# A quarter of a Q projection moved into seven-product runs, with the helper sums spread out to make room

## The chip, the cores and the metric

One core of one Trainium2 chip. The metric is the device time of one execution in microseconds (us). Each trace is of one execution. Engines: PE is TensorE (PEld its weight loads), DVE is VectorE, ACT is ScalarE, POOL is GpSimd, SP issues most transfers.

## The reference, cut to what matters

```python
def _A_ref(x, wqkv, wo):                       # x: 2048 tokens x 1024
    q, k, v = split(x @ wqkv)                  # 32 heads of 32
    phi = lambda t: jnp.where(t > 0, t + 1, jnp.exp(t)) + 1e-6
    pq, pk = phi(q), phi(k)
    kv = einsum("bhsd,bhse->bhde", pk, v)      # linear attention
    o = einsum(pq, kv) / (einsum(pq, pk.sum(s)) + 1e-6)
    return o @ wo
h = x + _A_ref(_layernorm(x), wqkv, wo)
h2 = h + mlp_over_tokens(_layernorm(h), w1, b1, w2, b2)   # 2048 -> 3584 -> 2048, gelu
```

The change lies in `x @ wqkv` and what surrounds it. The MLP, which takes more than half of the time, it leaves alone except in the last microseconds. Its two matrix products are called Mixer 1 (with w1) and Mixer 2 (with w2, also "the second MLP" below); psI are the accumulators of their inner products, hst the statistics of a block of h, and tp a transposed block.

## The kernel before: the parts that the change touches

A block product of 2x2 blocks normally takes 8 products. The kernel computes most of K and V in "runs" of 7 products (p1 to p7), at the price of sums of blocks: four of the weights (`w_sums`, T1 to T4, made once) and four of the tokens (`x_sums`, made for each pair of token blocks). All of these sums are VectorE's. TensorE accumulates into four buffers (psA, psB, psC, psE); results of different products are added on VectorE. The Q projection is plain: 32 "units" of 8 matmuls of 512 columns, some used as filler in the first run and the rest in a stage behind the K and V runs.

```python
def x_sums(q):                                    # 4 additions of 128x512 on VectorE
    a11, a12, a21, a22 = x_blocks(q)
    sm = spool.tile([P, 4, hk2, P], FP16, tag="xs", name="xs")
    pin(nc.vector.tensor_tensor(sm[:, 0], a21, a22, ALU.add))
    pin(nc.vector.tensor_tensor(sm[:, 1], sm[:, 0], a11, ALU.subtract))
    ...                                           # cut: sm[:, 2], sm[:, 3]
def p6(self): self.mm(self.B, self.s2, self.t2, False)   # needs sm[:, 1] and T2

def run_step(n, prev, after6=None, after5=None, after7=None, fill=None):
    n.p1()                                        # n: this run, prev: the run before
    prev.late22(); prev.p3(); prev.dve22(); prev.p4()
    n.p6()
    prev.dve21()
    if after6 is not None: after6()               # norm statistics of a later token block
    n.p2(); n.p5()
    prev.late12()                                 # Exp and Relu on ScalarE
    n.dve11()
    prev.dve12()                                  # last phi of the run before, on VectorE
    if after5 is not None: after5()
    n.p7()                                        # includes an addition on VectorE
    if after7 is not None: after7()               # x_sums of the next pair, after V runs
```

`pin` keeps an instruction in the order in which it is written. What is not pinned, such as the plain Q units in the first run, the builder may move. Accumulators outside the runs come from a ring of five buffers, handed out in turn, one for each call of `acc_tile`.

## Time and profile before

| | before |
|---|---|
| time, median of 3 | 560.86 us (560.84 to 561.08) |
| span of the profiled execution | 559.3 us |
| a K+V pair of runs | 13.03 us |
| first K run's first product starts at | 41.23 us |
| first Mixer 1 product (after the output projection) starts at | 234.10 us |
| last w2 load of the second MLP, issue to landing | 503.17 to 510.9, 7.8 us |
| start of the last group of psC matmuls to the end of the span | 7.70 us |

TensorE is the bound; the prediction below shows the lines for that. The short list of all that TensorE waited for (us in total, times, longest):

```profile
PE acc_t L98 <- DVE warm L88: 1.2, 1, 1.2
PE psB L945 <- DVE xs L931: 0.3, 1, 0.3
PE tp L1112 <- DVE xn L848: 0.2, 1, 0.2
```

The first is the program's start. There is one short wait on a token sum (at 34.31 us), one on a normalised block, and nothing else in 559 us.

### The profile page before, as it was taken

To read this page: it belongs to the slowest core of one execution; us is meant where nothing else is said; L and a number is where in the kernel's file an instruction comes from. 1 tells how busy PE (TensorE), PEld (TensorE's weight loads), DVE (VectorE), ACT (ScalarE), POOL (GpSimd) and SP (SyncE) were. 2 spreads that over 40 slices of the span, in tenths; PEclk is the share of its full clock that TensorE was granted. 3 is DMA by queue.
4 is the path that set the end of the run, shared out by engine and by line. 5 is a ranking of instruction groups with operands and counts; after the bars stand their busy time and mean duration, and the time that the engine had idled before them with its cause. 6 is when DMAs were issued, how large, how long until landed. Compare 5 with 4: busy or idle time off the path is not lost.

```text
span 559.3 us, 8827 instructions
## 1 busy us (share of the span) xinstructions
PE 553.0 (99%) x3339; PEld 316.2 (57%) x3339; DVE 435.3 (78%) x848; ACT 291.1 (52%) x617; POOL 28.0 (5%) x38
## 2 busy tenths in 40 slices
PE   8999999999999999999999999999999999999996
PEld 3444444454444444456766766666444667667664
DVE  6898888544777688889989789887997879749745
ACT  5747677766767877646456465464210413413222
POOL 1000000000000000000000000000002103103112
PEclk9999999999999999999999999999999999999999
DMA  9933342115774762102240440413869649849334
GB/s 306 297 76 76 80 90 39 19 36 203 223 203 136 241 202 76 75 1 85 69 150 5 147 134 18 151 46 88 206 203 237 197 137 245 206 131 229 86 95 66
DMA packets 83627, 74.25 MB, mean 133 GB/s; under 512 B 15602, under 2 KB 76032, under 8 KB 83584
## 3 DMA queue, kind: packets, MB, share of 16 engines
q1 hardware_dynamic: 78528, 69.09, 41.1%
q0 software_dynamic: 4384, 3.95, 5.3%
q10 hardware_dynamic: 672, 0.66, 0.3%
q8 instruction: 26, 0.43, 0.3%
q14 instruction: 17, 0.14, 0.1%
HBM read 58.86 MB, written 11.67 MB: 126 GB/s over the span
## 4 chain that ended last, share of the span: by engine, by line
PE 97%; DVE 2%; ACT 1%; issue 0%; DVEq 0%
PE psI L230 25%; PE acc_t L230 18%; PE psC L230 16%; PE psB L230 8%; PE psB L945 4%; PE psC L945 4%; PE psA L945 4%; PE acc_t L869 2%; PE acc_t L1231 2%; PE psB L342 2%; PE psA L342 2%; PE psE L945 2%; PE psC L342 2%; PE psA L230 1%; PE kvps L898 1%; PE psE L342 1%
## 5 line engine op out<-in xcount | busy, mean ns | idle before, releaser
L230 PEld LDWEIGHTS <-is 128*128 128x128 f16 x736 | 71.8, 98 | 31.2 <-DVE hi L230 0.4
L230 PEld LDWEIGHTS <-sa 128*128 128x128 f16 x606 | 59.2, 98 | 27.1
L230 PEld LDWEIGHTS <-wq 128*128 128x128 bf16 (+1 forms) x496 | 48.5, 98 | 28.1 <-issue 1.0
L230 PE MATMUL acc_t<-wo_sb,pqT 128*128 128x512 f16 x256 | 55.6, 379 | 0.0
L488 POOL DMA_DIRECT2D out_dram<-wq x30 | 26.1, 927 | 525.4 <-ACT wq L491 495.0
L230 PE MATMUL acc_t<-xnT,wq_sb 128*128 128x512 bf16 x192 | 43.4, 379 | 0.0
L230 PEld LDWEIGHTS <-pqT 128*128 128x128 bf16 x256 | 25.0, 98 | 30.5 <-issue 0.6
L193 DVE TENSOR_SCALAR e_sb<-e_sb 128x512 bf16<-128x512 bf16 x64 | 18.6, 290 | 28.7 <-ACT e_sb L189 28.1
L230 DVE TENSOR_TENSOR t<-psI,t 128x256 f32<-128x256 f32 (+1 forms) x45 | 20.8, 475 | 22.2 <-PE psI L230 20.9
L189 ACT ACTIVATE e_sb<-acc_t 128x512 bf16<-128x512 f32 x40 | 23.9, 597 | 24.5 <-PE acc_t L230 12.0
L230 PE MATMUL psC<-gs,wq 128*128 128x512 f16 x140 | 34.1, 379 | 0.0
L945 PEld LDWEIGHTS <-xs 128*128 128x128 f16 x208 | 20.0, 98 | 23.4 <-DVE xs L931 1.3
L230 PEld LDWEIGHTS <-wq_sb 128*128 128x128 bf16 x192 | 18.5, 98 | 23.0 <-issue 1.3
L230 PE MATMUL psC<-hT,sa 128*128 128x512 f16 x112 | 31.2, 379 | 0.0
L230 PE MATMUL psI<-hi,is 128*128 128x256 f16 x200 | 30.0, 273 | 0.0
L230 PE MATMUL psB<-hT,sa 128*128 128x512 f16 x112 | 29.7, 379 | 0.0
L230 DVE BATCH_NORM_STATS2 hst<-acc_t 128x6 f32<-128x512 f32 x32 | 21.4, 692 | 9.0 <-ACT h_bf L230 8.9
L945 PE MATMUL psA<-wkv,xnT 128*128 128x512 bf16 x104 | 26.7, 379 | 0.0
L945 PEld LDWEIGHTS <-xnT 128*128 128x128 bf16 x156 | 15.2, 98 | 18.5 <-issue 0.2
L230 PE MATMUL psC<-hT,wq 128*128 128x512 f16 x96 | 24.6, 379 | 0.0
L230 ACT CAST h_bf<-acc_t 128x512 bf16<-128x512 f32 x32 | 18.4, 582 | 11.9 <-PE acc_t L230 11.5
L230 ACT COPY psI<-psI 128x256 f32<-128x256 f32 x50 | 18.0, 360 | 11.6 <-PE psI L230 9.7
(229 smaller groups left out, 1090.2 us busy)
## 6 DMA issues: line engine op xcount, KB each, us to landing
wq<-in_B_w_dram SPq DMA_DIRECT2D x14, 1024.0 KB, 8.0
wq<-in_B_w_dram SPq DMA_DIRECT2D x12, 896.0 KB, 7.1
gs<-parked SPq DMA_DIRECT2D x9, 896.0 KB, 4.6
xr<-in_A_x_dram SPq DMA_DIRECT2D x16, 256.0 KB, 5.9
rdb<-rd_dram SPq DMA_DIRECT2D x32, 128.0 KB, 3.8
out_dram<-h_bf SPq DMA_DIRECT2D x16, 256.0 KB, 2.0
x_sb<-in_A_x_dram SPq DMA_DIRECT2D x15, 256.0 KB, 3.0
out_dram<-wq POOLq DMA_DIRECT2D x30, 128.0 KB, 4.7
```

The costliest lines, as they stand in the source:

```text
L189: pin(nc.scalar.activation(e_sb[:], src, ACT.Exp))
L193: pin(nc.vector.tensor_scalar(e_sb[:], e_sb[:], 1.0, PHI_EPS, ALU.min, ALU.add))
L230: return (lambda *a, **kw: pin(op(*a, **kw))) if self.always or getattr(Held, self.key) else op
L342: pe.matmul(ps[:, cols], lhsT=lhs[:, k, :], rhs=mv(k)[:, cols], start=(start and k == 0), stop=(k == self.nk - 1), skip_group_check=True,)
L488: nc.gpsimd.dma_start(to, ot[:, a:b], accum_op=ALU.add)
L869: mm = nc.tensor.matmul(pp[:, 0:CW], lhsT=xnT[:, kt, i * P:(i + 1) * P], rhs=wkv[:, kt, c * CW:(c + 1) * CW], start=(kt == 0), stop=(kt == ...
L898: pin(nc.tensor.matmul(kv_ps[b][:, sl, :], lhsT=pks[i % NPK][:, j * P:(j + 1) * P], rhs=vaugs[i % NVA][:, j, :], start=False, stop=(i == N ...
L945: pin(nc.tensor.matmul(ps[:], lhsT=lhs[:, k, :], rhs=rhs[:, k, :], start=(start and k == 0), stop=(k == hk2 - 1), skip_group_check=True,))
L1231: nc.tensor.matmul(qp[:, 0:SW], lhsT=wq_sb[:, kt, j * P:(j + 1) * P], rhs=xnT[:, kt, u * SW:(u + 1) * SW], start=(kt == 0), stop=(kt == ND ...
```

## The change

The intent: make tokens 1024 to 1535 of Q with seven products too, as two Q runs beside the K and V runs of q = 5 in the code, with Q's weight sums made one at a time, behind p7's addition in the K runs of four pairs. For buffer room T1 is written over the weight block that it is made from, and later buffers share memory. To save ScalarE work, a Q run's second phi takes its Relu inside a VectorE operation ("lean"). The last two stores by accumulating DMA become a fetch, an addition and a plain store.

```diff
-    for out, a, b in ((t1, b12, b11), (t2, b22, t1), (t3, b22, b12), (t4, b21, t2))[part]:
+    for out, a, b in ((t3, b22, b12), (t1, b12, b11), (t2, b22, t1), (t4, b21, t2))[part]:
     # cut: t1 is now a view of b12 itself; shared_sb holds sums, later rd, rdb and xr
+class QRun(KRun):                  # cut: 2 x (7 x 4 x 2) matmuls of 256 columns
+    lean = True
 def run_step(...):
     ...
     prev.late12()
     n.dve11()
-    prev.dve12()
     after5()
     n.p7()
+    prev.dve12()
     after7()
-q_units = [(u, j) for u in range(NSC) for j in range(ND)]
+q_units = [(u, j) for u in (0, 1, NSC - 1) for j in range(ND)]
+q_sums = {2: slice(0, 1), 3: slice(1, 2), 4: slice(2, 3), 5: slice(3, 4)}
-    for R in (KRun, VRun):
+    runs = [KRun(q), VRun(q)]
+    if q == 5:
+        runs = [runs[0], QRun(q // 2, 0), runs[1], QRun(q // 2, 1)]
+    # after7 of K runs: w_sums(qmov, q_sums[q]); of the second Q run: x_sums(q + 1, ...)
+if q == 6: ...                     # reload of the half of wq that was overwritten
-sums_at, ahead = (11, 13, 17, 19, 21), first_sums()
-scale_at = {7: (0, 0), 8: (0, 1), 15: (1, 0), 16: (1, 1), 23: (2, 0)}
+sums_at, ahead = (9, 11, 12, 13, 15), first_sums()
+scale_at = {7: (0, 0), 8: (0, 1), 14: (1, 0)}
     # cut: order of the denominators and scalings in the output stage; the tail
```

## The prediction

> **What bounds the kernel now.** I read the engine totals first, then the 40 slices, then who waited for TensorE, then the order of time in the two places where TensorE was not full.
>
> ```profile
> span 559.3 us, 8827 instructions
> ...
> PE 553.0 (99%) x3339; PEld 316.2 (57%) x3339; DVE 435.3 (78%) x848; ACT 291.1 (52%) x617; POOL 28.0 (5%) x38
> ...
> PE   8999999999999999999999999999999999999996
> ...
> PE 97%; DVE 2%; ACT 1%; issue 0%; DVEq 0%
> ```
>
> TensorE is busy 99% of the span and 97% of the chain that ended last. A busy TensorE need not be at its peak, so I checked spacing in the chain in order of time: 16 matmuls of 128x512 take 3.45 us (216 ns each), 8 of 128x256 take 0.87 us (109 ns each). Those are even spacings with no holes, and the granted clock is 1.00 everywhere. So time comes off only where TensorE gets fewer columns, and goes on wherever TensorE is made to wait. The second thing to know is where it waits already:
>
> ```profile
> 26.00:36.00 10.00, 9.72 (x57) 4.86 (x56) 9.39 (x16) 4.66 (x11) 0.00 (x0) 1.00 0.41 83
> 50.60:63.60 13.00, 13.00 (x73) 6.42 (x72) 10.56 (x25) 9.62 (x21) 0.00 (x0) 1.00 0.36 80
> 102.00:115.00 13.00, 13.00 (x74) 6.40 (x72) 6.77 (x17) 8.89 (x17) 0.00 (x0) 1.00 0.10 18
> 135.00:178.20 43.20, 43.20 (x217) 19.24 (x217) 30.04 (x64) 32.08 (x61) 0.00 (x0) 1.00 0.61 180
> 178.20:235.00 56.80, 56.80 (x270) 25.52 (x269) 45.59 (x93) 41.30 (x97) 0.00 (x0) 1.00 0.43 146
> ```
>
> After the window and its length the columns are PE, PEld, DVE, ACT, POOL, clock, DMA. Only the first stretch (start of the seven-product runs) has a TensorE hole, 0.28 us, and VectorE is 94% busy there. The others, a K+V pair early, a K+V pair late, the stage of plain Q units, and the output stage, have TensorE full and VectorE at 81, 52, 70 and 80%.
>
> In order of time there (start, duration, engine, source line, operation, output and inputs, shapes; in brackets the idle time before it and what ended it):
>
> ```profile
> 26.86 1.22 DVE L919 TENSOR_TENSOR wo_sb<-wkv 128x2048 f16<-128x2048 bf16 x1
> 28.11 1.23 DVE L919 TENSOR_TENSOR wo_sb<-wkv,wo_sb 128x2048 f16<-128x2048 bf16 x1
> ...
> 30.70 1.17 DVE L919 TENSOR_TENSOR wo_sb<-wkv 128x2048 f16<-128x2048 bf16 x1
> 31.79 1.22 DVE L919 TENSOR_TENSOR wo_sb<-wkv,wo_sb 128x2048 f16<-128x2048 bf16 x1
> ...
> 33.83 0.42 DVE L931 TENSOR_TENSOR xs<-xs,xnT 128x512 f16<-128x512 f16 x1
> ...
> 34.31 1.04 PE L945 MATMUL psB<-wo_sb,xs 128*128 128x512 f16 x4 [0.28 <-DVE xs L931]
> ```
>
> VectorE makes four V weight sums, then the token sums, and product 6 of the first V run starts the moment the second token sum ends. That is the spot with no slack at all.
>
> **What the Trainium skill says.** "TensorE: Matmul & The Clock Gate", Back-to-back issue gap, gives N/2.4 + 2.5 ns warm: 216 ns for 512 columns, 109 for 256. The trace agrees with both; it does not agree with the same section's 131 ns for sustained 512-column streams. Step-by-step there says matmuls stay in program order and only weight loads are pulled ahead; so a matmul that waits for VectorE holds all behind it, unless the instruction stream was ordered otherwise when it was built. "VectorE: DVE Perf Modes", Side-by-side, gives about 1224 ns for a two-tensor operation on 2048 16-bit elements; the weight sums take 1.22 to 1.23 us. "ScalarE: Activation LUTs", What ACT_TABLE_LOAD costs, gives 186 + 0.833 N ns with overlap of some 93 ns: 0.61 us each, 0.52 apart, at N = 512; here Exp takes 0.60 and follow-ons start 0.49 to 0.54 apart.
>
> **The change, part by part.**
> 1. Products. A quarter of Q is 8 units of 8 matmuls of 512 columns: 64 x 216 = 13.82 us. It becomes two runs of 7 products x 4 x 2 = 112 matmuls of 256 columns: 112 x 109 = 12.21 us. All on the path: -1.6 us. A weight load takes 98 ns and must fit beside each 109 ns; the inner products of the later stages, also 256 columns, show that it does.
> 2. ScalarE and VectorE in the runs. A Q run needs 3 copies, 4 Exp and 2 Relu, about 5 us, beside 6.1 us of TensorE. The step in which K's late activations meet Q's own adds up to some 6.1 us, just full, but its neighbours (K/V 9.6 of 13) have room. VectorE: additions 2 x 0.6, two phi of 0.73 and two of about 0.9 (the Relu is now a maximum inside an fp32 operation, which I cost like the 0.69 us addition): 4.5 us per Q run. Each of the four Q weight sums is 1.22 us in a pair that has 13.0 - 10.6 = 2.4 us to spare. No TensorE wait expected; 0.1 us allowed.
> 3. The stage of plain Q units shrinks from 24 units to 16, 13.8 us less room for nearly the same side work. VectorE there: 16 phi x 0.73 + 8 copies x 0.60 + 3 scalings x 1.13 + 4 sums x 1.13 + 1.46 = 25.9 of about 29.4 us (43.2 - 13.8), 88%. It lags a microsecond at the end, but ScalarE, not VectorE, frees most of the five accumulators. The output stage takes on two scalings (2.3 us) with 11 us idle; a delayed statistic of 1.2 us still leaves the next seed before its matmul. Allowed: 0.1 us.
> 4. Start of the runs, the dangerous part. T1 is now written over the b12 block in place. So T1 and T2 of K cannot be made while plain units still read K's weights, and V's T1, T2 come after the last plain V unit and, in the new order, after all four token sums. Before, from 26.86 to 34.25 VectorE did 4 weight sums, statistics, normalisation and 2 token sums ahead of product 6. After: 5 weight sums (K T1, T2, V T3, T1, T2) and 4 token sums. The additions are 1.13 + 2 x 0.36 = 1.85 us. The sum taken out earlier (at 19.69) does not help, as VectorE was waiting for ScalarE at 25.84 to 26.40 anyway. Product 6 is ready at about 36.1 instead of 34.3: up to +1.85 us, more than part 1 gains.
>    What can hide it: the plain Q unit behind product 2 has no data to wait for except an accumulator, which ScalarE frees at 34.21. Its matmuls are not pinned in order, while those of the runs are; the builder moved the equally unpinned PSUM clears up from behind the token sums to 22.2 us. If it moves this 1.73 us unit into the hole, 0.1 us of the cost is left.
> 5. Tail. The two stores by accumulating DMA (issued at 552.61 and 553.4, 3.7 us to landing) become a fetch, an addition and a plain store. The end is set by the plain stores after the last matmul, the last issued at 555.9. Less traffic beside them: -0.2 us.
> 6. The reload of half of wq (1 MB; such loads took 13.3 us) is issued some 25 us before its first use: hidden.
>
> Sum with the unit moved: 560.86 - 1.6 + 0.1 + 0.2 - 0.2 = 559.4. Without: 561.1.
>
> **Rivals.**
> (a) VectorE takes TensorE's place at the start and nothing fills the hole: 561.1, the gain gone. For it: the token-sum wait is already there, and the chain in order of time runs through those sums. Against: an unpinned unit is at hand. I give it 30 to 35%.
> (b) The Q runs stall, because ScalarE is full in the K-to-Q step and one accumulator of each kind serves all runs: 0.2 to 0.5 us in each of three steps, about 560.5. Against: in the K step the copy into the next accumulator has 0.4 us or more to spare, and V steps give the time back. 10%.
> (c) The shortened Q stage makes VectorE the bound, so that TensorE waits for fold copies or for the first mixer sums: 1 to 3 us, up to 562. Against: 88% and five accumulators. 8%.
> (d) The narrow matmuls go slower than 109 ns, since their moving operand is two 128-column pieces a stride apart: at 120 ns the gain would be 0.4 us and the time 560.6. I found nothing before that reads its moving operand so. 7%.
>
> **Range and chances.** The largest gain the arithmetic allows is about 1.8 us, 0.3%; two per cent is 11.2 us, which no part can give, and as a loss would need all rivals at once. Weighting 559.4 more than 561.1, I put 559.6; 558.7 to 561.4 holds both outcomes. Faster by over 2%: 0.005. Within: 0.98. Slower: 0.015.
>
> **What would show it.** Part 1: 112 matmuls of 128x256 near the fifth K and V runs, 8 in 0.87 us, and 64 fewer plain ones. Part 4: the second V product 6 (into psB) of the first run at about 36 us; either a plain Q unit ahead of it and hardly any wait, or a TensorE wait of some 2 us on a VectorE weight sum. Parts 2 and 3: no new TensorE waits on psA, psC or acc_t. Tail: two accumulating stores fewer, the span's last matmul to its end 0.2 us shorter than 4.8. I am wrong if TensorE idles over 0.5 us anywhere but at the start, if 8 narrow matmuls take over 0.9 us, or if the time lies under 558.7.

## The result, and the profile after

The changed kernel took 562.56 us (median of 3, 561.98 to 562.74) against 560.86, a ratio of 1.0027 with a 95% interval of 1.0004 to 1.0049. It is slower, by less than 2%; the prediction was 559.6, with a range of 558.7 to 561.4. Ratios here and below are the mean time of one kernel's fast runs over the mean of the other's in the same rounds, so not quite the ratio of the medians.

The page of the changed kernel, and the five stretches that the prediction showed for before (window, its length, then PE, PEld, DVE, ACT, POOL busy, clock, DMA share, GB/s):

```profile
span 560.8 us, 8925 instructions
...
PE 551.6 (98%) x3370; PEld 320.2 (57%) x3387; DVE 442.1 (79%) x858; ACT 291.8 (52%) x619; POOL 26.3 (5%) x36
...
PE 85%; DVE 5%; ACT 2%; DMA 2%; issue 1%; DVEq 0%; ACTq 0%
```

```profile
26.00:36.00 10.00, 9.28 (x54) 4.50 (x53) 9.56 (x15) 3.97 (x10) 0.00 (x0) 1.00 0.41 83
50.60:63.60 13.00, 12.51 (x69) 6.12 (x70) 10.80 (x25) 9.07 (x21) 0.00 (x0) 1.00 0.32 72
102.00:115.00 13.00, 12.89 (x87) 8.47 (x87) 9.38 (x23) 8.70 (x18) 0.00 (x0) 1.00 0.36 103
135.00:178.20 43.20, 42.99 (x230) 19.53 (x233) 26.95 (x62) 30.07 (x56) 0.00 (x0) 1.00 0.58 180
178.20:235.00 56.80, 56.80 (x269) 25.37 (x267) 49.22 (x100) 41.62 (x98) 0.00 (x0) 1.00 0.65 201
```

TensorE is busy 1.4 us less, but the span is 1.4 us longer (560.78 against 559.35 before rounding). The chain shows that something is wrong: TensorE's share of it fell from 97% to 85%. In the windows, the early K+V pair (50.6 to 63.6), which was full, now has a hole of 0.49 us although VectorE is only 83% busy there. (The 0.21 us missing in 135 to 178.2 is no hole: at four places there one matmul's record is missing from the trace.) The list of waits names the new holes:

```profile
PE psB L968 <- DVE xs L957: 1.6, 4, 0.4
PE acc_t L98 <- DVE warm L88: 1.2, 1, 1.2
PE psA L234 <- DVE hst L234: 0.5, 1, 0.5
PE psC L968 <- DVE kt L1065: 0.3, 1, 0.3
PE psI L234 <- DVE is L234: 0.3, 1, 0.3
PE acc_t L1294 <- ACT r_sb L191: 0.2, 1, 0.2
...
PE psB L234 <- ACT psB L531: 0.2, 1, 0.2
...
```

Two lines of 0.2 us are cut: the wait for a normalised block that was there before, and one at the start that some traces of both kernels have.

In order of time (start, duration, engine, line, operation, in brackets the idle time before it and what ended it), the places with a gap, and one Q product:

```profile
34.14 0.81 PE L1294 MATMUL acc_t<-xnT,wq_sb 128*128 128x512 bf16 x3 [0.23 <-ACT r_sb L191]
35.38 1.04 PE L968 MATMUL psB<-wo_sb,xs 128*128 128x512 f16 x4 [0.44 <-DVE xs L957]
...
37.12 1.24 PE L1294 MATMUL acc_t<-xnT,wq_sb 128*128 128x512 bf16 x5
...
57.90 1.04 PE L968 MATMUL psB<-shared_sb,xs 128*128 128x512 f16 x4 [0.38 <-DVE xs L957]
...
88.54 1.04 PE L1105 MATMUL psA<-xnT,wq_sb 128*128 128x256 bf16 x8
89.41 1.03 PE L968 MATMUL psB<-wkv,xs 128*128 128x512 bf16 x4
...
116.00 1.02 PE L968 MATMUL psC<-shared_sb,xnT 128*128 128x512 f16 x4 [0.32 <-DVE kt L1065]
...
235.71 3.61 PE L234 MATMUL psA<-hE,wq 128*128 128x512 f16 x16 [0.47 <-DVE hst L234]
...
515.67 0.94 PE L234 MATMUL psI<-gi,is 128*128 128x256 f16 x7 [0.26 <-DVE is L234]
...
523.60 2.10 PE L234 MATMUL psB<-gT,sa 128*128 128x512 f16 x9 [0.18 <-ACT psB L531]
```

A bracket is shorter than the loss. Four matmuls start 0.865 us apart from the next four, so the true cost is how far the next start lies behind that spacing: at 57.90 it is 0.55 us, not 0.38. The Q product at 88.54 is followed by the next at 89.41: 8 matmuls of 256 columns in 0.87 us, exactly as predicted.

Read this way, from one milestone to the next, the 1.43 us between the two profiled spans come from:

| where | after minus before, us | measured as |
|---|---|---|
| Q's products | -1.61 | 112 matmuls of 256 columns for 64 of 512, even spacing |
| start of the runs | +0.54 | first K run at 41.65 instead of 41.23, with 0.12 us won just before |
| three K+V pairs | +1.66 | 13.58 instead of 13.03 us each, product 6 of the K run waits for a token sum |
| K run behind the Q runs (q = 6, called the seventh below) | +0.48 | product 4 at 116.00 instead of 115.52 |
| end of the output projection | +0.47 | psA waits for a statistic |
| last w2 load, second MLP | +0.83 | lands 9.6 us after its issue instead of 7.8; psI starts 0.41 us late, and the matmuls into psB at 523.60, which wait for ScalarE, 0.42 more |
| tail | -0.92 | 6.78 instead of 7.70 us from the start of the last psC group on |
| rest | 0.0 | |

The wait of psB at 523.60 is put down to the late load because it stands in every trace with a late w2 load told of below and in none without. Why each of these waits came is a theory as long as it is only read. The experiments follow.

### The profile page after: what moved, and what is told of

It is laid out like the page before. It is cut to its first block, busy times and chain, and to the rows that moved or that the text cites. A ratio compares the mean times of both kernels' runs of the same rounds, so it can differ in the third digit from the quotient of the medians.

```text
span 560.8 us, 8925 instructions
## 1 busy us (share of the span) xinstructions
PE 551.6 (98%) x3370; PEld 320.2 (57%) x3387; DVE 442.1 (79%) x858; ACT 291.8 (52%) x619; POOL 26.3 (5%) x36
## 4 chain that ended last, share of the span: by engine, by line
PE 85%; DVE 5%; ACT 2%; DMA 2%; issue 1%; DVEq 0%; ACTq 0%
PE psI L234 23%; PE psC L234 14%; PE acc_t L234 14%; PE psB L234 8%; PE psB L968 4%; PE psA L968 3%; PE psC L968 3%; PE psB L346 2%; PE psA L346 2%; PE acc_t L1294 2%; PE psE L968 2%; DMA wq<-in_B_w_dram 2%; PE psC L346 2%; PE psA L234 1%; PE psE L346 1%; DVE is L234 1%
## 5 line engine op out<-in xcount | busy, mean ns | idle before, releaser
L492 POOL DMA_DIRECT2D out_dram<-wq x28 | 24.4, 929 | 522.4 <-ACT wq L495 488.3
L234 PE MATMUL acc_t<-xnT,wq_sb 128*128 128x512 bf16 x125 | 29.3, 379 | 0.2
L189 ACT ACTIVATE e_sb<-acc_t 128x512 bf16<-128x512 f32 x32 | 19.1, 597 | 18.7 <-PE acc_t L1294 9.4
L234 DVE TENSOR_TENSOR e<-psI,es 128x256 f32<-128x256 f32 x20 | 8.5, 425 | 20.4 <-PE psI L234 20.4
L234 PE MATMUL psI<-gi,is 128*128 128x256 f16 x168 | 22.3, 273 | 0.3 <-DVE is L234 0.3
```

The costliest lines, as they stand in the source:

```text
L189: pin(nc.scalar.activation(e_sb[:], src, ACT.Exp))
L234: return (lambda *a, **kw: pin(op(*a, **kw))) if self.always or getattr(Held, self.key) else op
L492: nc.gpsimd.dma_start(to, ot[:, a:b], accum_op=ALU.add)
```

## The experiments

Theories: (1) the last phi of the previous run (`dve12`) was moved behind p7, so it now stands on VectorE ahead of the token sums; (2) VectorE is overfull in the step after the second Q run; (3) the ring of five accumulators is shifted by the 8 `acc_tile` calls that are gone, so the first Mixer 1 product gets the buffer that was freed last; (4) a fetch of instructions by DMA falls into the last w2 load and makes it late. The rival of all of them is the general one: VectorE has more to do, so everything is later.

Each time below is the median of 4 to 6 timed executions, of which the ratio, with its 95% interval, is taken against runs of the kernel before on the same chip (its medians there: 560.96 to 561.17).

### Token sums ahead of the phi

```diff
     n.p7()
-    prev.dve12()
     after7()
+    prev.dve12()
```

> The changed kernel with one order undone: in a run step the token sums (x_sums) go ahead of the last phi of the run before (dve12), the addition stays ahead of both. Theory 1 (the phi that the change moved behind the addition now stands between the addition and the token sums, and product 6 of the next K run waits for them): the three waits of 0.55 us before psB at the K runs 3, 4 and 5 go, 1.6 to 1.7 us off, about 560.9 us against 562.56. Rival (VectorE is simply overfull there because of the 1.22 us Q weight sums, and whatever order it works in, something is late): under 0.5 us off, and TensorE waits somewhere else in the same pairs.

Measured: 561.07 us, ratio 1.0005 (0.9993 to 1.0018), span 559.7. The waits of psB on xs in the pairs are gone. What VectorE does ahead of product 6, in the changed kernel:

```profile
55.70 0.69 DVE L1039 TENSOR_TENSOR vaug<-psC,e 128x512 bf16<-128x512 f32 x1
...
56.30 0.28 DVE L194 TENSOR_SCALAR e_sb<-e_sb 128x512 bf16<-128x512 bf16 x1
...
56.62 0.42 DVE L198 TENSOR_TENSOR pk<-e_sb,r_sb 128x512 bf16<-128x512 bf16 x1
56.97 0.42 DVE L957 TENSOR_TENSOR xs<-xnT 128x512 f16<-128x512 bf16 x1
57.42 0.42 DVE L957 TENSOR_TENSOR xs<-xs,xnT 128x512 f16<-128x512 f16 x1
```

and with the sums first:

```profile
55.62 0.69 DVE L1039 TENSOR_TENSOR vaug<-psC,e 128x512 bf16<-128x512 f32 x1
...
56.22 0.41 DVE L957 TENSOR_TENSOR xs<-xnT 128x512 f16<-128x512 bf16 x1
...
56.67 0.42 DVE L957 TENSOR_TENSOR xs<-xs,xnT 128x512 f16<-128x512 f16 x1
...
57.27 1.03 PE L968 MATMUL psB<-shared_sb,xs 128*128 128x512 f16 x4
```

The phi of 0.28 + 0.42 us between the addition and the sums is the whole delay: the second sum ends at 57.84 with it and at 57.09 without, and product 6 wants to start at 57.3. In the kernel before, the same phi ran at 53.9 to 54.8, where VectorE was waiting for ScalarE anyway:

```profile
53.88 0.29 DVE L193 TENSOR_SCALAR e_sb<-e_sb 128x512 bf16<-128x512 bf16 x1 [0.76 <-ACT e_sb L189]
...
54.40 0.43 DVE L194 TENSOR_TENSOR pk<-e_sb,r_sb 128x512 bf16<-128x512 bf16 x1 [0.23 <-ACT r_sb L190]
```

The first Mixer 1 product starts 1.46 us earlier than in the changed kernel (234.25 instead of 235.71), although its own wait grew from 0.5 to 0.7. Theory 1 holds.

### The same move alone, in the kernel before

```diff
-    prev.dve12()
     after5()
     n.p7()
+    prev.dve12()
     after7()
```

> The kernel before with nothing but that phi moved behind the addition of product 7. Theory 1: the same waits appear without any Q weight sum: four pairs (token sums for runs 3 to 6) have the layer norm between, so up to 4 x 0.45 = 1.8 us slower, 562.3 to 562.9. Rival (the Q weight sums are needed for it): within 0.3 us of 560.86.

Measured: 563.27 us, ratio 1.0036 (1.0023 to 1.005), with no Q run and no Q sum in it.

```profile
PE psB L945 <- DVE xs L931: 1.8, 5, 0.4
...
PE tp L1112 <- DVE xn L848: 1.0, 1, 1.0
```

One of the five waits is that of the start, as before; the other four are product 6 of four K runs, 0.38 us in the trace and 0.55 in spacing each. Four times 0.55 is 2.2 us, and the time rose by 2.3. (The 562.3 to 562.9 expected had counted 0.45 a wait, so it fell short.) (The 1.0 us on tp is a wait for the first loads in the profiled execution alone.) The move costs without any Q sum, so the rival "more work" is not needed.

### The phi back where it was, with the Q runs

```diff
     n.dve11()
+    prev.dve12()
     after5()
     n.p7()
-    prev.dve12()
     after7()
```

> The changed kernel with the last phi of a run back where the kernel before had it, ahead of the sixth product's work instead of behind the seventh's. Theory 1: the three waits of psB on xs (1.2 us of the 1.6) go as with x sums ahead, -1.5 us, 561.1 us; but the sixth product's and the additions' VectorE work then stand behind a 0.9 us lean phi in the steps after Q runs, which cost up to 0.9 in the step of the seventh K run: 561.1 to 562. Rival (the move was needed for the Q runs): as slow as the changed kernel or slower, 562.6 or more, with new waits of psC or psE in the 100 to 120 us stretch.

Measured: 562.47 us, ratio 1.0021 (1.0008 to 1.0033), above the range expected. The three pairs give their 1.66 us back, but 1.0 us of it is lost again beside the Q runs:

```profile
115.61 1.02 PE L968 MATMUL psC<-shared_sb,xnT 128*128 128x512 f16 x4 [0.90 <-DVE kt L1065]
```

The seventh K run's product 4 waits 0.90 us instead of 0.32 (0.57 us of the 1.0), and a product of the first Q run now waits 0.3 for an addition as well (0.43 us). The rest of the gain is gone by the end of the span too: in this execution the start was 0.27 us later, and psI waited 0.5 us for the last w2 load instead of 0.3. So the move of the phi had a purpose: a lean phi ahead of p7's addition delays the steps after Q runs. Its price was paid in all the steps where it was not needed. Putting the token sums ahead of it keeps that purpose and removes the waits in the pairs; the wait of 0.3 us behind the Q runs stays.

### The norm of block 15 one step earlier

```diff
     i = {"K": 2 * q + 3, "V": 2 * q + 4}.get(kind, NS)
+    if kind == "Q" and n.half == 1:
+        i = 2 * q + 5
+    elif kind == "K" and q == 6:
+        i = NS
```

> The changed kernel with the norm statistics of token block 15 moved from the step of the seventh K run to the step of the second Q run. Theory 2 (VectorE has 6.7 us of work in that 6.05 us step, and the seventh K run's fourth product waits 0.32 us for it and starts 0.48 us late): the wait of psC on kt is gone, and the seventh K run's fourth product starts 5.5 to 5.6 us after the run's start instead of 6.0; the time is 562.1. Rival (the wait is the lean phi's own length, which stays): the wait stays at 0.3, time unchanged or the Q run's step becomes longer instead.

Measured: 562.56 us, ratio 1.0032 (1.002 to 1.0045), no faster.

```profile
114.78 1.03 PE L968 MATMUL psB<-wkv,xs 128*128 128x512 bf16 x4
115.64 0.59 PE L968 MATMUL psC<-shared_sb,xnT 128*128 128x512 f16 x2
```

The step itself is mended: product 4 follows product 3 after 0.86 us, and the list of waits has no psC line. The local 0.48 us is there, so theory 2 holds for that step; the time does not show it. The profile says where part of it went: the last w2 load landed 9.8 us after its issue, and psI waited 0.5 instead of 0.3. A gain ahead of a wait for a load is partly eaten by the wait. The rest is below what these timings resolve: the changed kernel itself, timed again with an edit that turned out to change nothing (below), gave 563.2.

### The ring of accumulators: turned by three, then by four

```diff
 sums_at, ahead = (9, 11, 12, 13, 15), first_sums()
+for _ in range(3):                 # and range(4) in the second
+    acc_ring.append(acc_ring.pop(0))
```

> The changed kernel with the ring of accumulator pools turned by three places before the plain Q units, so that the seeds of the output stage lie in the pools where they lay before (8 units fewer is 3 places modulo 5). Theory 2 (the 0.47 us wait of the first mixer product for the last statistics is a matter of which PSUM bank psA reuses, not of VectorE being later): the wait goes, 0.4 to 0.5 us off. Rival (VectorE ends the output stage later because of the two scalings it took on): no change, within 0.15 us.

Measured: 562.76 us, ratio 1.0034 (1.0022 to 1.0047); psA still waited 0.5. The experiment missed: in the built program the last block's second half still lay in the first Mixer 1 product's buffer, so it tested nothing. The buffers that the built program assigns told which turn would free it: four.

> The changed kernel with the ring of accumulator buffers turned by four at the start of the output stage, so that the first Mixer 1 product's buffer is one that the statistics of token blocks 13 and 14, and not the last block's, hold. Theory 3 (the 0.47 us before that product is the last block's statistic, which holds its buffer): the wait of psA on hst is at most 0.1 us instead of 0.47, and the time is 562.1, 0.4 to 0.5 under the changed kernel (562.6). Rival (the statistics as a whole are late, whatever the buffer): the wait stays at 0.4 to 0.6, time unchanged.

Measured: 562.34 us, ratio 1.0024 (1.0011 to 1.0037).

```profile
231.65 3.62 PE L234 MATMUL acc_t<-wo_sb,pqT 128*128 128x512 f16 x16
235.10 1.67 PE L234 MATMUL psA<-hE,wq 128*128 128x512 f16 x7
```

The product follows the output projection in step, and no wait of psA is left. VectorE had the same work in the same order; only which buffer came round had changed. Theory 3 holds. The clock time fell by only 0.2, and once more psI's wait for the load grew, from 0.3 to 0.6.

### The start: a shorter way to T2

```diff
-for out, a, b in ((t3, b22, b12), (t1, b12, b11), (t2, b22, t1), (t4, b21, t2))[part]:
-    pin(nc.vector.tensor_tensor(out, a, b, ALU.subtract))
+for out, a, b, op in ((t3, b22, b12, sub), (t2, t3, b11, add), (t1, b12, b11, sub), (t4, b21, t2, sub))[part]:
+    pin(nc.vector.tensor_tensor(out, a, b, op))
```

> The changed kernel with only the start mended: V's T2 as T3 + W11, so two sums instead of three stand before the first V run's fourth-sum product. Expected from the four-repair run, whose first K run starts at 41.22 us instead of 41.65: this product starts at 34.2 to 34.4 instead of 35.38, the first K run's start is 0.4 us earlier, time 562.1 to 562.2. Rival (the hole is filled by plain Q matmuls anyway, so nothing is gained): start within 0.1, time 562.6.

Measured: 562.54 us, ratio 1.0029 (1.0016 to 1.0041). Product 6 starts at 34.23 instead of 35.38 us, and the first K run at 41.15 instead of 41.65. Locally 0.5 us, in the time nothing that can be told from noise, with psI's wait for the load at 0.5.

### The tail alone, in the kernel before

```diff
-t = odd[self.p - 2][:, 0:2, :].rearrange(...)
+t = odd[self.p - 2][:, 6 * dh:6 * dh + 2, :].rearrange(...)
-    r = 2 + 2 * (a > 0)
+    r = 6 * dh + 2 + 2 * (a > 0)
+    st.fetch(0, 1)
     st.fetch(1, 0)
```

> The kernel before with only the tail of the change: the two accumulating stores of the last pair become fetch, addition, plain store. From the traces, last 14-matmul product to the end of the span is 7.48 us before and 6.63 after: theory 3 says 0.85 us faster, about 560.0. My prediction had 0.2 us. Rival (the end differs from run to run by that much): no change beyond 0.2 us.

Measured: 560.27 us, ratio 0.9987 (0.9975 to 1.0), span 558.5 and 6.8 us from the last group (551.66) to the end instead of 7.70. The tail is worth 0.7 us by the medians and 0.9 by the traces. The rival is out: over all traces told of here that stretch took 7.3 to 8.0 us in the five with the old tail and 6.8 in each of the fifteen with the new one.

### The late w2 load: first TensorE's instruction fetches

Instructions come by DMA too: two queues of the page's list, q8 and q14, are of kind "instruction". Which engines they serve had to be found out. The list of transfers inside the span of the last w2 load (from its issue to its landing) has for the kernel before one line of a load and no instruction queue:

```profile
wq<-in_B_w_dram SPq DMA_DIRECT2D x1, 896.0 KB, 7.8
```

and for the changed kernel two fetches inside:

```profile
q8 instruction: 1, 0.02, 0.6%
q14 instruction: 1, 0.01, 0.2%
...
wq<-in_B_w_dram SPq DMA_DIRECT2D x1, 896.0 KB, 9.6
```

The changed kernel has 96 more matmuls and weight loads, so q8, which brings 16 KB at a time (26 fetches for the 6678 matmuls and weight loads of the kernel before, some 257 each), comes earlier. The first test put more instructions into the kernel before, and no more columns:

```diff
-    for t in range(n):
-        mm(warm[:, 0:P], warm[:, 0:BANK])
+    for t in range(4 * n if n == 6 else n):
+        mm(warm[:, 0:P], warm[:, 0:P if n == 6 else BANK])
```

> The kernel before with its first six warm-up matmuls of 512 columns cut into 24 of 128 columns: 36 more TensorE instructions and the same columns, so that every later fetch of TensorE's instructions falls some 2.5 us earlier in the program. Theory 4 (the last w2 load of the second MLP lands late where such a fetch falls inside it): the fetch now at 511.6 us comes at about 509, inside the load issued at 503.2, which lands 9.5 to 10 us after its issue instead of 7.8, and TensorE waits 0.4 to 0.7 us more there; time 561.3 to 561.7. Rival (the load is late for the kernel's other changes, or by where it starts): it lands after 7.5 to 8.2 us, no wait, time 560.8 to 561.1.

Measured: 560.87 us, ratio 1.0002; the load landed after 7.7 us. The fetch had moved only from 8.4 to 7.9 us after the issue, still behind the landing, so the place that it was meant for was not tested. But its profiled execution, at 562.51 us the slowest of the five, shows a loss elsewhere: psI waits 0.6 us at 474.92. There the w2 load issued at 463.55 landed after 10.0 us; in eighteen of the nineteen other traces this load took 7.9 to 8.4 us. TensorE lost 1.2 us by it. TensorE's fetch began only 8.4 us after that issue, when the load had landed in those traces. So a load can be late with no such fetch in its first 8 us, for a reason that the record doesn't show, and one trace of a late load is weak evidence for what made it late.

The second cut all ten warm-ups into eight:

> The kernel before with all ten of its warm-up matmuls of 512 columns cut into eight of 64: some 140 more TensorE instructions, because 36 moved the fetch near the last w2 load only from 8.4 to 7.9 us after the load's issue, still behind its landing at 7.7. The changed kernel's 97 more had it at 6.5. Theory 4 (a fetch of TensorE's instructions inside the load makes it land late): the fetch comes 5 to 7 us after the issue, the load lands after 9.5 to 10 us, TensorE waits 0.3 to 0.7 us, time 561.3 to 561.8. Rival (a): the other queue's 8 KB fetch, which does not move here, is what delays it: the load lands after 7.7 to 8.2 us, no wait, time 560.8 to 561.2. If narrow warm-ups leave TensorE's clock lower at the start, that shows in the first 15 us and is taken off.

Measured: 564.7 us, ratio 1.0067 (1.0054 to 1.008).

```profile
PE tp L1112 <- DVE xn L848: 1.8, 2, 1.6
PE psI L230 <- DVE is L230: 1.7, 1, 1.7
```

The fetch did not fall where I had put it but 1.6 us ahead of the last load's issue, inside the load before it. That one took 7.6 us instead of 5.4, the last one 11.0 instead of 7.8, and TensorE waited 1.7 us. The only edit is that of the warm-ups: more TensorE instructions, each of fewer columns. So it fits that such a fetch makes loads late, though the place was not the predicted one; 1.2 us of the time was lost before the first K run (the first line, early loads; the granted clock of the first 20 us was 1.00).

### VectorE's instruction fetch in the kernel before

```diff
-    nc.vector.memset(m4[:], 0.0)
+    for _ in range(17):
+        nc.vector.memset(m4[:], 0.0)
```

> The kernel before with 16 more tiny memsets on VectorE in the gap ahead of the first block's statistics (1.2 us idle there). In the changed kernel VectorE has 14 more operations, and the 8 KB fetch near the last w2 load comes 6.2 us after the load's issue instead of 8.6. Theory 4b (that 8 KB fetch is VectorE's and is what delays the load): it comes 5 to 7 us after the issue, the load lands after 9.5 to 10 us, TensorE waits 0.3 to 0.7 us there, time 561.3 to 561.7. Theory 4 (TensorE's fetch, which does not move here): the load lands after 7.7 to 8.2 us, time 560.9 to 561.1.

Measured: 561.08 us, ratio 0.9999, load 7.6 us. The 8 KB fetch on q14 moved by 10 us, which shows that it brings VectorE's instructions, but to 1.3 us ahead of the last load's issue, not into the load. Of the 17 fetches on q14 within the span eight moved, by 4 to 21 us, and nine stayed within 0.6, so q14 serves other engines as well; the fetch near the last w2 load is one of VectorE's.

### Moving TensorE's fetch out of the load, in the changed kernel

> The changed kernel with 12 of its plain Q units (tokens 1536 to 2047, and half of tokens 512 to 1023) as two matmuls of 256 columns in place of one of 512: 192 more TensorE instructions, the same columns, so that TensorE's fetches fall some 4 to 7 us later against the program near the last w2 load (a fetch brings 256 of them: 192 more is like 64 fewer). Theory 4: no fetch inside the load issued at about 504.7; it lands after 7.5 to 8.2 us instead of 9.6, the wait of psI on it is gone, time 561.8 to 562.2 (-0.3 to -0.7). Rival (the load is late by what else the changed kernel issues, or narrow matmuls cost as much as is gained): it lands after 9.5 us or the time is 562.5 or more.

> The four repairs and the 192 more TensorE instructions. Theory 4: the last w2 load lands after 7.5 to 8.2 us instead of 10.0, psI's wait of 0.64 is gone, time 559.3 to 559.5, 0.5 to 0.7 under the mended kernel of this call and 1.5 under the kernel before (ratio 0.997). Rival: the load stays late, time as the mended kernel's.

Both cut matmuls in a routine that those Q units no longer pass through, so the built programs had not one instruction more. They served as repeats: the changed kernel 563.2 us (ratio 1.0045, 1.0032 to 1.0058; one of the five, 564.64, at a granted clock of 0.997), and the kernel with four repairs 559.91 (0.9984, 0.9972 to 0.9996). The next two did it in the output projection:

```diff
+hw = CW // 2 if i < 6 else CW
 for j in range(ND):
-    ht.matmul(seeds[i][dc][:, 0:CW], lhsT=..., rhs=wf[:, j, dc * CW:(dc + 1) * CW], ...)
+    for h in range(0, CW, hw):
+        ht.matmul(seeds[i][dc][:, h:h + hw], lhsT=..., rhs=wf[:, j, dc * CW + h:dc * CW + h + hw], ...)
```

> The changed kernel with the first six of 16 token blocks of the output projection as two matmuls of 256 columns in place of one of 512: 192 more TensorE instructions (6962 rows of the built program against 6770), the same columns. Theory 4 (a fetch of TensorE's instructions inside the last w2 load makes it late): the fetch that came 6.5 us after that load's issue comes at 10 us or later, the load lands after 7.5 to 8.2 us instead of 9.6, the wait of psI on it is gone, time 0.5 under the changed kernel's (561.9 to 562.6, as its repeats gave 562.6 and 563.2). Rival: the fetch moves and the load still lands after 9.5 us.

Measured: 562.57 us, ratio 1.0029 (1.0014 to 1.0043). TensorE's fetch moved from 6.5 to 8.0 us after the issue, and psI's wait is gone from the list, but the time is that of the changed kernel (562.56). The load landed after 9.5 us, not 7.7. Theory 4 as I had put it (TensorE's fetch alone) falls.

### Both fetches moved, and four repairs together

The four repairs (token sums ahead of the phi, block 15's norm earlier, the ring turned by four, T2 from T3) were run alone, then with TensorE's fetch moved, then with 16 more tiny memsets on VectorE.

> The changed kernel with four repairs together: x sums ahead of the last phi (known: -1.5), the norm of block 15 one step earlier (-0.48), the ring turned by four (-0.47), and at the start V's second weight sum taken from the third one as T3 + W11, with T1 behind the second product, so that the sum that the first K run needs is not third in the row (-0.5). The sum of theories 1 to 3 and the start: 562.6 - 2.95 = 559.6 us, ratio to the kernel before 0.9976. The late w2 load stays (+0.68). If a repair only uncovers another wait: 560 to 561.

Measured: 559.98 us, ratio 0.998 (0.9967 to 0.9994), span 558.3.

> The kernel with the four repairs once more, on this chip: 559.8 to 560.1 us, the last w2 load landing after 10 us with psI waiting 0.6.

Measured: 560.33 us, ratio 1.0005 (0.9983 to 1.0027). Two of the six executions, 564.11 and 562.97 us, had a granted clock of 0.994 and 0.997; the other four took 559.8 to 560.58. Load 9.9 us, psI waiting 0.5.

> The four repairs and these 192 instructions. Theory 4: the load lands after 7.5 to 8.2 us instead of 9.8 to 10, psI's wait of 0.4 to 0.6 is gone, time 559.3 to 559.5 (the mended kernel's three results: 559.98, 559.91, 560.33). Rival: the load stays late and the time is 559.9 to 560.3.

Measured: 559.48 us, ratio 0.9972 (0.9959 to 0.9985). In the span of the last w2 load (502.0 to 511.4):

```profile
q8 instruction: 1, 0.02, 0.6%
q14 instruction: 1, 0.01, 0.2%
...
wq<-in_B_w_dram SPq DMA_DIRECT2D x1, 896.0 KB, 9.4
```

> The mended kernel with its fetch of TensorE moved, and with 16 more tiny memsets on VectorE at the start, which move the 8 KB fetch from 6.0 us after the issue of the last w2 load to some 4 us before it. Theory 4b (that fetch inside the load makes it late in the changed kernel): the load lands after 7.5 to 8.2 us instead of 9.4, VectorE's wait of 0.55 for it is gone; the time stays at 559.3 to 559.7, since TensorE no longer waits there. Rival (neither fetch is the cause): it lands after 9.3 us or more and VectorE waits 0.5.

Measured: 559.31 us (559.17 to 560.27), ratio 0.9967 (0.9953 to 0.998). In the span of the load (502.5 to 510.2) there is no instruction queue any more:

```profile
wq<-in_B_w_dram SPq DMA_DIRECT2D x1, 896.0 KB, 7.7
```

VectorE no longer waits for the load, nor TensorE for VectorE there. With sixteen tiny memsets more at the start of the program a load 500 us later landed 1.7 us earlier. Between 512 and 521 us that saves TensorE 0.61 us in the trace. The time does not show it: 559.31 on chip 2 and 559.48 on chip 13, with intervals of the ratio that overlap. Programs side by side, us from the issue of the last w2 load:

| kernel | TensorE's fetch starts | VectorE's fetch starts | load landed |
|---|---|---|---|
| before | 8.4 | 8.6 | 7.8 |
| before, tail alone | 8.5 | 9.2 | 8.1 |
| before, phi late | 8.8 | 8.7 | 7.8 |
| before, first warm-up split | 7.9 | 8.6 | 7.7 |
| before, 16 memsets | 8.4 | -1.3 | 7.6 |
| before, second warm-up split | -1.6 | 8.9 | 11.0 |
| changed | 6.5 | 6.2 | 9.6 |
| changed, token sums first | 6.7 | 6.3 | 10.0 |
| changed, TensorE's fetch moved | 8.0 | 6.3 | 9.5 |
| four repairs, TensorE's fetch moved | 7.9 | 5.9 | 9.4 |
| four repairs, both moved | 7.8 | -12.4 | 7.7 |

The nine traces that the table leaves out are of the changed kernel and its repairs: VectorE's fetch at 5.8 to 6.4 us in all of them, the load after 9.8 to 10.0. So it was late in all thirteen traces with that fetch inside, and in the changed kernel's family on time in the one without it (the last two rows differ by 16 memsets, and by the chip). That points to VectorE's fetch, with one execution on the other side. TensorE's, at 6.3 to 7.2 instead of 7.9 or 8.0, may add 0.2 to 0.6. In the second warm-up split it would have to be TensorE's.

For TensorE's fetch the twenty traces hold better evidence: the second of the two loads of w2 into `w2o` that are issued close together at 480 to 484 us. It took 12.2 to 12.4 us in the twelve traces in which a fetch of TensorE's began 7.5 to 8.1 us after its issue, and 10.6 to 11.2 in the eight in which it began 9.5 us or more after it. Three pairs that differ in the number of TensorE's instructions fall on both sides: before and second warm-up split (11.2 and 12.3), changed with and without the fetch moved (11.2 and 12.3), four repairs likewise (11.0 and 12.3). These 1.2 us are about the length of the fetch, 0.9 to 1.0. TensorE did not wait there.

Not settled: by what mechanism an 8 KB fetch that takes 0.3 us on one of 16 DMA engines costs 1.7 us, and why one that falls 1.3 us ahead of the issue, also within the load before, costs nothing. In the changed kernel the rate of all transfers falls to 43 and 26 GB/s some 9 us after the load's issue, so only a small part of the load was then still under way. Each row is one profiled execution.

## Why the prediction was wrong, point by point

**Part 1, the products: right.** 8 narrow matmuls take 0.87 us; -1.61 us, as the sum had it. Rival (d) is out.

**Part 2, VectorE in the runs: this is the step that failed.** It said "No TensorE wait expected; 0.1 us allowed", from the share of VectorE that was free in a pair; it did not ask in which order VectorE works. The diff moves one phi behind p7's addition in every step, and I read over that line: a move that adds nothing to the sum of work. The runs show +1.66 us in three pairs of the changed kernel and, in the kernel before with that move alone, 2.2 us in four. VectorE had 2.2 us to spare in such a pair (13.0 - 10.8); what mattered was 0.7 us at one place in its order. On top, the step after the second Q run was overfull by 0.48 us. I had looked at that squeeze on ScalarE (rival b, 0.2 to 0.5 us in a step) and not on VectorE, so rival (b) had the size of that loss, but not its cause.

**Part 3, the Q and output stages: half right.** The shortened Q stage lost nothing (no wait in the list lies in it), so rival (c) is out. The output stage was to lose at most 0.1, since "a delayed statistic of 1.2 us still leaves the next seed before its matmul". I followed the seeds and not the first product of the next stage, which takes whichever accumulator the ring gives it. That cost +0.47 us, and the wait is gone with the ring turned by four.

**Part 4, the start: the mechanism was right, the size lay between its two cases.** The builder did float the plain unit into the hole, but only 3 of its 8 matmuls (at 34.14; the other 5 stand behind product 2, at 37.12). It also put V's T1 ahead of all token sums and T2 between the first and the second, so product 6 started at 35.38 us, between the 34.3 and 36.1 that I had given. The cost was 0.54 where 0.1 was allowed for a filled hole. It was avoidable: T2 can be had from T3, and then product 6 starts at 34.23 and the first K run at 41.15 us.

**Part 5, the tail: direction right, undersized.** -0.2 predicted, -0.7 to -0.9 measured by itself.

**Part 6, the reload: right.** No wait on it anywhere.

**Not foreseen:** the last w2 load, +0.83 us, most likely from a shift of instruction counts. Nothing in my list of rivals looked beyond the stages that the diff touches.

The signed sum: -1.61 - 0.92 was to be had; +1.66 + 0.48 + 0.54 + 0.47 + 0.83 went on top, of which I had allowed 0.3. With all of these repaired, the kernel takes 559.31 us, 0.3% under the kernel before. That this is close to my 559.6 is luck: the prediction had left out both the losses and most of the tail.

## What to carry to other kernels

When TensorE is full, do not ask whether another engine has room in a stage, but what stands ahead of the one result that the next pinned matmul needs; read every moved line of a diff as carefully as every added one. Read a gain of half a microsecond from the stage that it is in, and then ask what waits further on, since a load or a buffer behind it may eat it. The ring step alone gave 0.2 of its 0.47 us, and the norm and the start alone nothing that the timings resolve. Where a full kernel gets slower in a stage that nobody touched, look at which buffer a ring hands out there, and at whether instruction fetches have moved into a load.

## What the Trainium skill lacked or had wrong

- "TensorE: Matmul & The Clock Gate", Back-to-back issue gap: its figure of 131 ns for a sustained stream of 512-column matmuls is seen nowhere; the streams here are 216 ns apart, and those of 256 columns 109 ns, also with a moving operand of two 128-column pieces.
- "Runtime: NRT & Kernel Launch", Instruction fetch mechanics, says that a DMA queue refills an engine's instructions in blocks of 16 KiB. Here the fetches on q8 bring 16 KB and those on q14 8 KB. No page says that such fetches can make a kernel's loads late. Runs: a w2 load of 896 KB lands after 7.6 to 8.1 us with no fetch in it, after 9.4 to 10 us with VectorE's 8 KB fetch about 6 us into it.
- "DMA: Bandwidth & Descriptors", Queues, rings and completion order, says that each engine takes its queues in turn, a packet at a time, and names row 14 as internal to the runtime, refills among its uses. That fits a delay of the fetch's own length: 0.31 us for 8 KB on q14, 0.9 to 1.0 for 16 KB on q8. The 1.7 us between the last two rows of the table above are more than five times that, so the page's account doesn't cover it. TensorE's instructions come on q8 here.
- No page gives how far one more instruction moves these fetches: 16 on VectorE moved eight of them by 4 to 21 us, 36 on TensorE moved one by 0.5 us near the load and two others by 7 us.
